# Second MoE layer as Strassen half products in four sum banks, with attention regrouped to 256 queries

## Chip, cores, metric

One Trainium2 chip, one core. The metric is the device time of one execution in microseconds (us); the span in a profile is a little shorter (413.1 against 414.8 here).

## What is computed

Attention over 4 batches of 8 heads of 768 queries (head size 64), then a mixture of 4 experts on the 3072 rows that come out. Three heads are "retrieval" heads (plain causal mask); five are "streaming" heads (4 sink keys and a window of 64).

```python
mask = where(retrieval[h], causal, causal & (is_sink | in_window))
a = softmax(where(mask, q @ k.T / 8, -1e9))          # (4, 8, 768, 768)
x = (a @ v).transpose(0, 2, 1, 3).reshape(3072, 512)
p = probs / (probs.sum(-1, keepdims=True) + 1e-9)    # (3072, 4)
for e in range(4):
    out += p[:, e:e+1] * (relu(x @ w1[e]) @ w2[e])   # 512 -> 1024 -> 512
```

## The kernel before

It works in 8 groups of 384 queries. While TensorE runs the experts of one group, the attention of the next group is threaded through it in small steps. The program fixes the order of instructions on every engine by the order in which it issues them. The kernel divides PSUM, where TensorE's results arrive, into eight banks of 512 fp32 columns: four for scores and first layer, two for attention values, two for the second layer's outputs.

```python
def bank():
    return pA.tile([P, 512], FP32, name="pA", bufs=4)

def scores(h):
    for cols, parts, masks in score_tiles(h):
        # ... matmuls keys x queries into a bank, exp on ScalarE, mask on VectorE
        es_of[h].append((es, parts))
        run_late()                      # products of earlier values, if any wait
        yield ns

def values(h):
    hp, u = divmod(h, 2)
    # ... (first group: other banks, warm-up matmuls)
    ps = pV.tile([P, 512], FP32, name="pV", bufs=2)
    # ... matmuls: values and a column block of ones, so sums stand beside them
    nc.scalar.activation(out=rc[r, :], in_=ps[o, 0:CH], func=AF.Ln, bias=eps[o, :])

    def scale(r=r, ps=ps):
        nc.vector.tensor_tensor(
            out=xT[g][r, hp, :], in0=ps[r, 0:CH], in1=rc[r, :], op=ALU.mult)

    # ... (pairs of the first group cut)
    nc.scalar.activation(out=rc[r, :], in_=rc[r, :], func=AF.Exp, scale=-1.0)
    late.append(scale)                  # issued at the next score step

def moe_group(g):
    for e in range(E):
        # ... layer 1: for each of 8 blocks 4 matmuls of 384 columns, ReLU on ScalarE
        for j in range(3):
            ps_o = pO.tile([P, DM], FP32, name="pO", bufs=2)
            for ft in range(FTP):
                nc.tensor.matmul(out=ps_o, lhsT=hs[:, ft, j * P : (j + 1) * P],
                                 rhs=w2sb[:, e * FTP + ft, :],
                                 start=(ft == 0), stop=(ft == FTP - 1))
            # ... acc = p * ps_o (+ acc) on VectorE, store after the last expert
```

The softmax here doesn't subtract the row's maximum and nothing guards it: scores larger than these inputs give would overflow.

Of the kernel before, what the change touches and what calls it, by code (L numbers as in the profile page):

```python
# [17 lines left out]
def kernel(  # L18
# [28 lines left out]

    nc = tc.nc
# [3 lines left out]
    CH = 3 * P  # L52
# [7 lines left out]
    G = B * NCH  # L60

    RETR = (1, 0, 1, 0, 0, 0, 1, 0)
    RH = [h for h in range(H) if RETR[h]]
    SH = [h for h in range(H) if not RETR[h]]
    NS = int(n_sink)
    NW = int(window)
    TK = 96
    R0 = P - TK
    TQ = TK + NW
    NT = S // TK  # L70
    TC = CH // TK
    assert NS <= R0 and NW == 64 and NS + NW <= TK
    WQ = 55
    WK = WQ + NW - 1
    WT = 7
    WO = P - WK + NW
    assert WT * WQ - 1 == CH and NS + WK <= P

# [3 lines left out]
    pA = ctx.enter_context(tc.tile_pool(name="pA", bufs=1, space=bass.MemoryType.PSUM))  # L82
    pV = ctx.enter_context(tc.tile_pool(name="pV", bufs=1, space=bass.MemoryType.PSUM))
    pO = ctx.enter_context(tc.tile_pool(name="pO", bufs=1, space=bass.MemoryType.PSUM))
# [7 lines left out]
    def bank():  # L92
        return pA.tile([P, 512], FP32, name="pA", bufs=4)


    w1sb = pers.tile([P, E * DMP, F], FP16, name="w1sb")
    w2sb = pers.tile([P, E * FTP, DM], FP16, name="w2sb")
    NR, NSH = len(RH), len(SH)
    kR = []
    kSf = []  # L100
    vR = []
    vSf = []
    for i in range(2):
        kR.append(pers.tile([P, NCH, NR, 3, P], FP16, name=f"kR{i}"))
        kSf.append(pers.tile([P, NCH * TC * NSH * P], FP16, name=f"kS{i}"))
        vR.append(pers.tile([P, S // P, len(RH), P], FP16, name=f"vR{i}"))
        vSf.append(pers.tile([P, NT * NSH * P], FP16, name=f"vS{i}"))
    kS = kSf[0].rearrange("p (c t s x) -> p c t s x", c=NCH, t=TC, s=NSH)
    vS = vSf[0].rearrange("p (t s x) -> p t s x", t=NT, s=NSH)

    def windows(x, c):

        return x[1 - c][:, 0 : WT * NSH * P].rearrange(
            "p (t s x) -> p t s x", t=WT, s=NSH
        )
# [5 lines left out]
    bS = pers.tile([P, 3, TQ], FP16, name="bS")  # L121
    eps = pers.tile([P, 1], FP32, name="eps")
    mC = pers.tile([P, 2 * P], FP16, name="mC")
    mS = pers.tile([P, 4, TQ], FP16, name="mS")
    mW = pers.tile([P, WT + 2, WQ], FP16, name="mW")
# [4 lines left out]


    kRr = pers.tile([P, NR, 3, P], FP16, name="kRr")
    kSr = pers.tile([P, WT, NSH, P], FP16, name="kSr")
    k_sinks = pers.tile([NS, 1, NSH * P], FP16, name="k_sinks")
    v_sinks = pers.tile([NS, 1, NSH * P], FP16, name="v_sinks")

# [5 lines left out]
    def key_tile(b, c, h, t):  # L142

        i = b % 2
        if RETR[h]:
            return kR[i][:, t // 3, RH.index(h), t % 3, :]
        if b:
            return windows(kSf, c)[:, t, SH.index(h), :]
        return kS[:, t // TC, t % TC, SH.index(h), :]

    def v_tile(b, c, h):

        i = b % 2
        if RETR[h]:
            return vR[i][:, :, RH.index(h), :]
        if b:
            return windows(vSf, c)[:, :, SH.index(h), :]
        return vS[:, :, SH.index(h), :]


    q16 = {}

    def rows_of(x, b, h, c):
        return x[b, h, c * CH : (c + 1) * CH, :].rearrange("(j p) d -> p j d", p=P)

    def tiles_of(x, b, h, c):
        return x[b, h, c * CH : (c + 1) * CH, :].rearrange("(t r) d -> r t d", r=TK)

    def windows_of(x, b, h, c):

        assert b > 0
        first = ((b * H + h) * S + c * CH - WO) * D
        return bass.AP(x.tensor, x.offset + first, [[D, P], [WQ * D, WT], [1, D]])

    def load_by_rows(x, x16, b, c):
        for j in range(3):
            s0 = c * CH + j * P
            gp.dma_start(
                out=x16[:, j, :, :],
                in_=x[b, :, s0 : s0 + P, :].rearrange("h p d -> p h d"),  # L180
            )

    def load_q(b, c):
        q16[b, c] = att.tile([P, 3, H, D], FP16, name="q16", bufs=2)
        load_by_rows(q, q16[b, c], b, c)

    def load_triples(x, dst, b, c):

        gp.dma_start(
            out=dst.rearrange("p h j d -> p h (j d)"),  # L190
            in_=x[b, :, c * CH : (c + 1) * CH, :].rearrange(
                "h (p j) d -> p h (j d)", j=3
            ),
        )

    def load_k(b, c):

        for h in range(H):
            if RETR[h]:
                gp.dma_start(  # L200
                    out=kRr[:, RH.index(h), :, own(h)], in_=rows_of(k, b, h, c)
                )
            else:
                gp.dma_start(  # L204
                    out=kSr[:, :, SH.index(h), own(h)],
                    in_=windows_of(k, b, h, c),
                )
# [3 lines left out]
    def alloc_qT(b, c):  # L211
        qTs[b, c] = att.tile([P, HP, CH], FP16, name="qT", bufs=2)

    def put_sinks(x, sinks, c):

        x = x.rearrange("p t s x -> p t (s x)")
        src = sinks
# [211 lines left out]
    for e in range(2, E):  # L429
        load_w1(e, 0, F)  # L430
        load_w2(e)
# [421 lines left out]
```

## Time and profile before

| | before |
|---|---|
| time, median of 3 runs | 414.85 us |
| span of the profiled run | 413.1 us |
| TensorE busy | 395.8 us (96%) |
| VectorE, ScalarE, GpSimd busy | 38%, 58%, 34% |
| mean granted TensorE clock | 0.998 |

The prediction below reads the groups, the chain and the windows. In the profile lines PE is TensorE, PEld its weight loads, DVE VectorE, ACT ScalarE, POOL GpSimd; L728 is line 728 of that run's kernel, so the numbers shift where a run adds lines. Of the tiles, pA is a bank of scores or layer 1, pV a value bank, es the exponentials, rc the reciprocals of their sums, xT the normalised values, hs the hidden activations, sums their sums. Two more views matter for comparing later. First the row of the page that gives the granted TensorE clock in tenths (9 is 90% or more), one digit for each fortieth of the span:

```profile
PEclk9999999999999999999999999999999999999999
```

Second, of the table of waits (engine, line, what it waited for: us in total, times, longest), TensorE's largest and the largest that concerns values:

```profile
PE pA L728 <- ACT hs L741: 2.5, 4, 0.7
PE pV L609 <- DVE es L583: 0.9, 1, 0.9
```

TensorE never waits for a value bank: with two banks, one head's values are written while the other's are read.

### The profile page before, as it was taken

Reading aid. Unit: us, or ns where it says so; the run is one execution under the profiler, and the core shown is the slowest. Engines: PE = TensorE matmul, PEld = TensorE weight load, DVE = VectorE, ACT = ScalarE, POOL = GpSimd, SP = SyncE. Lnnn points to the kernel's source line nnn. Section 1 sums busy time; section 2 is a strip of 40 time slices with the busy share of each in tenths; the row PEclk is TensorE's granted clock in tenths of the full one; section 3 lists DMA queues with packets and bytes.
Section 4 is the critical chain, followed back from the end, with each engine's and each line's share of the span. In section 5 each row is a group of like instructions: output and inputs, shape, how many; then the busy total and the mean of one; then the engine's idle time right before and its main releaser. Section 6 shows DMA issues by size and latency. Waiting matters only on the chain.

```text
span 413.1 us, 6801 instructions
## 1 busy us (share of the span) xinstructions
PE 395.8 (96%) x2670; PEld 222.4 (54%) x2670; DVE 155.8 (38%) x302; ACT 240.9 (58%) x509; POOL 141.7 (34%) x176
## 2 busy tenths in 40 slices
PE   6799999999999999999999999999999999999996
PEld 3565555555555555555555555555555555555552
DVE  7975553223433325233333333233343222432222
ACT  2676874336876547656665448566565477653331
POOL 8938618359359177002930085000000000000000
PEclk9999999999999999999999999999999999999999
DMA  9999999999989999058984999259002000020002
GB/s 173 142 195 204 209 208 133 136 210 124 174 64 181 217 75 101 27 107 147 111 53 96 182 72 77 17 108 166 2 2 76 5 2 0 2 76 2 1 2 76
DMA packets 159988, 40.83 MB, mean 99 GB/s; under 512 B 150364, under 2 KB 154836, under 8 KB 159956
## 3 DMA queue, kind: packets, MB, share of 16 engines
q0 software_dynamic: 102592, 20.98, 59.5%
q1 hardware_dynamic: 54164, 18.62, 21.7%
q10 hardware_dynamic: 3200, 0.79, 0.9%
q8 instruction: 21, 0.34, 0.3%
q14 instruction: 11, 0.09, 0.1%
HBM read 43.57 MB, written 6.29 MB: 121 GB/s over the span
## 4 chain that ended last, share of the span: by engine, by line
PE 86%; ACT 6%; DVE 4%; DMA 2%; issue 1%; ACTq 0%; DVEq 0%
PE pO L749 40%; PE pA L728 36%; PE pV L609 5%; PE pA L561 4%; ACT hs L741 2%; DMA q<-in_q_dram 2%; ACT rc L628 2%; DVE kS L490 1%; ACT rc L638 1%; DVE vS L261 1%; ACT es L579 1%; DVE kR L474 1%; DVE qT L465 0%; PE pO L355 0%; PE pV L355 0%
## 5 line engine op out<-in xcount | busy, mean ns | idle before, releaser
L728 PE MATMUL pA<-xT,w1sb 128*128 128x384 f16 x1024 | 187.4, 326 | 3.9 <-ACT hs L741 2.5
L749 PE MATMUL pO<-w2sb,hs 128*128 128x512 f16 x768 | 180.8, 379 | 0.0
L741 ACT ACTIVATE hs<-pA 128x384 f16<-128x384 f32 x256 | 122.1, 494 | 95.9 <-PE pA L728 89.1
L728 PEld LDWEIGHTS <-w1sb 128*128 128x128 f16 x1024 | 96.8, 98 | 65.5 <-issue 5.5
L749 PEld LDWEIGHTS <-hs 128*128 128x128 f16 x768 | 72.7, 98 | 74.3 <-ACT hs L741 0.6
L765 DVE SCALAR_TENSOR_TENSOR acc<-pO,p_sb,acc 128x512 f32<-128x512 f32 x72 | 53.9, 749 | 99.5 <-PE pO L749 98.9
L579 ACT ACTIVATE es<-pA 128x512 f16<-128x512 f32 (+3 forms) x122 | 61.0, 511 | 22.7 <-PE pA L561 20.9
L628 ACT ACTIVATE rc<-pV,eps 64x384 f32<-64x384 f32 x60 | 34.5, 575 | 33.0 <-PE pV L609 32.0
L204 POOL DMA_DIRECT2D kSr<-in_k_dram x30 | 30.1, 1006 | 36.5 <-issue 14.7
L250 POOL DMA_DIRECT2D vS<-in_v_dram x30 | 30.4, 1024 | 34.8 <-PE pV L609 34.0
L633 DVE TENSOR_TENSOR xT<-pV,rc 64x384 f16<-64x384 f32 x60 | 33.1, 552 | 4.2 <-PE pA L728 1.7
L583 DVE TENSOR_TENSOR es<-es,mW 128x384 f16<-128x384 f16 x30 | 10.8, 360 | 57.2 <-ACT es L579 57.2
L638 ACT ACTIVATE rc<-rc 64x384 f32<-64x384 f32 x58 | 30.2, 521 | 1.8
L761 DVE TENSOR_SCALAR acc<-pO,p_sb 128x512 f32<-128x512 f32 x24 | 18.0, 749 | 34.3 <-PE pO L749 33.0
L200 POOL DMA_DIRECT2D kRr<-in_k_dram x18 | 14.1, 783 | 47.2 <-DMA kR<-kRr 43.2
L583 DVE TENSOR_TENSOR es<-es,mC 128x256 f16<-128x256 f16 (+1 forms) x42 | 10.8, 257 | 45.4 <-ACT es L579 45.0
L561 PE MATMUL pA<-qT,kR 128*128 128x384 f16 (+2 forms) x120 | 25.0, 278 | 0.4
L609 PE MATMUL pV<-es,vR 128*128 128x384 f16 (+2 forms) x120 | 21.6, 278 | 0.0
L246 POOL DMA_DIRECT2D vR<-in_v_dram x24 | 19.2, 800 | 4.3 <-DMA w2sb<-in_moe_w_dram 4.2
L561 PEld LDWEIGHTS <-kS 128*128 128x128 f16 x255 | 13.9, 98 | 9.5 <-issue 2.9
L561 PE MATMUL pA<-qT,kS 128*128 128x55 f16 (+4 forms) x255 | 16.6, 195 | 2.2 <-ACT es L579 1.6
L609 PEld LDWEIGHTS <-vS 128*128 128x128 f16 x255 | 13.2, 98 | 9.1 <-DVE vS L261 3.0
(77 smaller groups left out, 161.3 us busy)
## 6 DMA issues: line engine op xcount, KB each, us to landing
out_dram<-acc SPq DMA_DIRECT2D x24, 256.0 KB
w1sb<-in_moe_w_dram POOLq DMA_DIRECT2D x4, 1024.0 KB, 14.5
w2sb<-in_moe_w_dram POOLq DMA_DIRECT2D x4, 1024.0 KB, 17.5
kSr<-in_k_dram POOLq DMA_DIRECT2D x30, 112.0 KB, 3.8
vS<-in_v_dram POOLq DMA_DIRECT2D x30, 112.0 KB, 3.8
q<-in_q_dram POOLq DMA_DIRECT2D x18, 128.0 KB, 4.4
vR<-in_v_dram POOLq DMA_DIRECT2D x24, 48.0 KB, 4.1
kRr<-in_k_dram POOLq DMA_DIRECT2D x18, 48.0 KB, 4.1
```

Source lines behind the costliest of these rows:

```text
L204: gp.dma_start(out=kSr[:, :, SH.index(h), own(h)], in_=windows_of(k, b, h, c),)
L250: gp.dma_start(out=t[:, :, own(h)], in_=windows_of(v, b, h, c))
L561: nc.tensor.matmul(out=ps[:, o : o + nq], lhsT=key_tile(b, c, h, t), rhs=qTs[b, c][:, hp, q0 : q0 + nq], start=(n == 0 or not first), stop ...
L579: nc.scalar.activation(out=es[:, 0:cols], in_=ps[:, 0:cols], func=AF.Exp, scale=SC)
L609: nc.tensor.matmul(out=ps[:, q0 : q0 + nq], lhsT=v_tile(b, c, h)[:, t, :], rhs=es[:, o : o + nq], start=(n == 0), stop=(n == len(work) - 1 ...
L628: nc.scalar.activation(out=rc[r, :], in_=ps[o, 0:CH], func=AF.Ln, bias=eps[o, :])
L633: nc.vector.tensor_tensor(out=xT[g][r, hp, :], in0=ps[r, 0:CH], in1=rc[r, :], op=ALU.mult)
L638: nc.scalar.activation(out=rc[r, :], in_=rc[r, :], func=AF.Exp, scale=-1.0)
L728: nc.tensor.matmul(out=pss[ft][:, 0:CH], lhsT=w1sb[:, e * DMP + ct, ft * P : (ft + 1) * P], rhs=xT[g][:, ct, :], start=(ct == 0), stop=(ct ...
L741: nc.scalar.activation(out=hs[:, ft, :], in_=ps[:, 0:CH], func=AF.Relu)
L749: nc.tensor.matmul(out=ps_o, lhsT=hs[:, ft, j * P : (j + 1) * P], rhs=w2sb[:, e * FTP + ft, :], start=(ft == 0), stop=(ft == FTP - 1),)
L765: nc.vector.scalar_tensor_tensor(out=acc[nt], in0=ps_o, scalar=p_ap, in1=acc[nt], op0=ALU.mult, op1=ALU.add,)
```

## The change

**Intent.** Strassen's scheme multiplies 2x2 blocks with seven half products in place of eight. The products are summed over the four experts in PSUM, so the additions that combine them are done once per group, not once per expert. For that the probability has to be in the hidden activations (scaled at the eviction of layer 1, on VectorE, one bank in four on ScalarE and GpSimd). Four banks hold the running sums through a whole group. Groups become 256 queries (2 x 128 rows), streaming heads use 52-query tiles, and all attention after the second group stays at fp16 loads and DMA transposes. The first two of twelve groups use a plain second layer while the weights' sums are made.

The eight banks are now three for scores and first layer, one for values, four for sums. Two heads share the value bank, 256 columns each. The core of the diff (cuts marked):

```diff
-    CH = 3 * P
+    NJ = 2
+    CH = NJ * P
...
-        return pA.tile([P, 512], FP32, name="pA", bufs=4)
+        return psum.tile([P, 512], FP32, name="pA", bufs=3)
+    def bank_v():
+        return psum.tile([P, 512], FP32, name="pV", bufs=1)
+    def bank_m(i):
+        return psum.tile([P, 512], FP32, name=f"pM{i}", bufs=1)
... attention, values of a head
+            if u == 0:
+                run_late()
+                ps_of[hp] = bank_m(hp - 1) if first and hp else bank_v()
+            ps = ps_of[hp][:, u * CH : (u + 1) * CH]
...
+            if u == 1:
+                # ... two logarithms, one exponential on ScalarE
+                def normalise(x=ps_of[hp], rc=rc):
+                    for w in (1, 0):
+                        r = rows[w]
+                        nc.vector.tensor_tensor(
+                            out=xT[g][r, hp, :], in0=x[r, w * CH : (w + 1) * CH],
+                            in1=rc[r, :], op=ALU.mult)
+                late.append(normalise)
... layer 1, eviction
+                    if i == 0:
+                        nc.scalar.activation(out=tmp, in_=ps, func=AF.Relu)
+                        gp.tensor_tensor(out=h4, in0=tmp4, in1=p4, op=ALU.mult)
+                    else:
+                        nc.vector.scalar_tensor_tensor(
+                            out=h4, in0=ps4, scalar=0.0, in1=p4,
+                            op0=ALU.max, op1=ALU.mult)
... sums of the hidden activations, per expert
+        add(hs[:, :, P:CH], hs[:, :, 0:P], s[:, 0:2], ALU.subtract)   # 1024 columns
+        add(hs[:, 0:FH, :], hs[:, FH:FTP, :], s[:, 2:4])              # 1024 columns
+        add(hs[:, 0:FH, 0:P], hs[:, FH:FTP, P:CH], s[:, 4])           # 512 columns
... second layer: 7 x 4 matmuls of 256 columns
+        m52, m34, m76, m1 = sum_banks[g]
+        for n, step in enumerate(steps):
+            for ps, half, a, b in step:
+                for f in range(FH):
+                    nc.tensor.matmul(out=ps[:, half * HD : (half + 1) * HD],
+                        lhsT=a(f), rhs=b(f),
+                        start=(e == 0 and f == 0 and half == 0),
+                        stop=(e == E - 1 and f == FH - 1))
+            if e == E - 1:
+                way_out(g, n)          # copies and five additions, one store
... order of a cycle
+    merge(plain(0, 0, 3), PLAIN_NS, 1, 0.0, 0.9)   # attention of group 1 beside one expert
+    # then seven plain experts with the attention of group 2, then per group:
+            yield from in_turns(layer1_scaled(g, 0), layer2(last, 2))
+            ...
```

## The prediction

> **What bounds the kernel now.** I read the page first (busy shares, groups), then the chain of work that ended last in order of time, then TensorE's timeline for the pitch of single matmuls, then ten-microsecond windows, then the timelines of the first 26 us and of the end.
>
> From the page, the busy shares and the two largest groups (columns: engine, busy us, share, instructions; line, operation, operands, count, busy us and mean ns, idle before):
>
> ```profile
> PE 395.8 (96%) x2670; PEld 222.4 (54%) x2670; DVE 155.8 (38%) x302; ACT 240.9 (58%) x509; POOL 141.7 (34%) x176
> ...
> L728 PE MATMUL pA<-xT,w1sb 128*128 128x384 f16 x1024 | 187.4, 326 | 3.9 <-ACT hs L741 2.5
> L749 PE MATMUL pO<-w2sb,hs 128*128 128x512 f16 x768 | 180.8, 379 | 0.0
> ...
> L765 DVE SCALAR_TENSOR_TENSOR acc<-pO,p_sb,acc 128x512 f32<-128x512 f32 x72 | 53.9, 749 | 99.5 <-PE pO L749 98.9
> ...
> L633 DVE TENSOR_TENSOR xT<-pV,rc 64x384 f16<-64x384 f32 x60 | 33.1, 552 | 4.2 <-PE pA L728 1.7
> ```
>
> TensorE is busy for 96% and its two MoE lines have next to no idle before them; VectorE is at 38%. The mean of a matmul includes its pipeline, so the cost has to come from pitches. The chain in order of time (start, length, what) gives them over unbroken runs, and the timeline gives the short ones:
>
> ```profile
> 70.54 5.20 PE pA L728 x32
> ...
> 121.31 1.73 PE pO L749 x8
> ```
> ```profile
> 122.88 0.36 PE L609 MATMUL pV<-es,vS 128*128 128x54 f16 x7
> 123.08 1.24 PE L749 MATMUL pO<-w2sb,hs 128*128 128x512 f16 x5
> ...
> 162.43 0.38 PE L561 MATMUL pA<-qT,kR 128*128 128x256 f16 x2
> 162.65 0.59 PE L749 MATMUL pO<-w2sb,hs 128*128 128x512 f16 x2
> ```
>
> So 384 columns cost 5.20/32 = 162.5 ns, 512 columns 216 ns, 256 columns 0.22/2 = 110 ns, and seven 54/55-column matmuls start within 0.20 us, 28.6 ns each. That is columns/2.4 + 2.6 ns, with a floor near 28.6 ns. The windows (span; busy us and count of PE, PEld, DVE, ACT, POOL; clock; DMA) show where TensorE is not full:
>
> ```profile
> 50.00:60.00 10.00, 9.13 (x70) 5.41 (x69) 6.33 (x14) 7.84 (x17) 1.74 (x2) 1.00 1.18 210
> ...
> 170.00:180.00 10.00, 10.00 (x64) 5.51 (x63) 3.56 (x6) 5.66 (x12) 1.02 (x1) 1.00 0.39 91
> ...
> 400.00:410.00 10.00, 8.96 (x48) 4.41 (x45) 2.25 (x3) 3.35 (x7) 0.00 (x0) 1.00 0.15 54
> ```
>
> From 70 us to 400 us it is full but for about 3 us in all. Pricing every matmul of the instruction order with the pitches gives 389.4 us (166.5 first layer, 165.8 second, 50.6 attention, 5.2 warm-up, 1.3 for the second half of fp32 transposes, three of which take 0.33 us in the timeline). So of the 413.1 us span 23.7 is TensorE without work: 10.3 before the first MoE matmul at 24.3 us, 9.2 between there and 408.9, and 4.2 after the last matmul. The time reported is 1.75 above the span.
>
> **What the skill says.** "TensorE: Matmul & The Clock Gate", section "Wait — 56ns, not 53.3ns?": start to start N/2.4 plus about 2.5 ns warm, and a floor near 25 ns for small N. The trace agrees on the first (162.5, 216) and shows 28.6 on the second. "VectorE: DVE Perf Modes", section "The perf-mode tier table": a 16-bit tensor_tensor in SBUF runs two elements a cycle, any with a PSUM operand one. The trace agrees: the fp16 mask products take 291 ns at 256 columns and 360 at 384 (0.54 ns a column), the 512-column fp32 operation on PSUM 749. "GPSIMD Engine Reference", section 3.1: a GpSimd tensor_tensor of 2048 fp32 took 4497 ns; no such operation is in this trace. "SBUF — State Buffer", section "SBUF: two separate sides": a VectorE operation with two SBUF inputs and a GpSimd operation reading SBUF exclude each other; not shown by this trace either, and it bears on the new sums against the new GpSimd multiply.
>
> **The change, part by part.**
>
> *Second layer.* Ten of twelve groups (the first two stay plain) take 7 x 4 half products of 256 columns per expert in place of 16 x 512: 10 x 4 x 28 x 109.2 ns = 122.3 us, against 640 x 216 = 138.2. That is -15.9. The seven-eighths rule would give -17.3; the 2.6 ns on twice as many matmuls takes the rest.
>
> *First layer.* The same columns in 1536 matmuls of 256 instead of 1024 of 384: 167.8 against 166.5, +1.3.
>
> *Attention.* Retrieval has the same columns in more matmuls. The streaming heads of the first batch go from 160-column tiles to five 48/52-column ones, at the floor of 28.6. Priced like before: 47.7 against 50.6, less 2.9; fp32 transposes +0.6. Warm-up 1.5 against 5.2, less 3.7.
>
> TensorE's work is then 369.0, against 389.4: -20.4. All of this is on the path, since TensorE sets the end. The rest of the question is how much idle comes with it.
>
> *Prologue.* Its 256 queries need less VectorE work, and VectorE set its length: busy with few gaps from 5.6 us on. After: kR 3 x 0.42, kS 5 x 1.0 (three pieces each), sinks 1.6, qT 1.25, value sinks 2.0, xT 8 x 0.42, together 14.5 us, by 0.15 us plus 1.04 ns a column from the 384-column rows. I take the first MoE matmul at 19.5 instead of 24.3. TensorE's work before it is 6.6, so 12.9 idle (+2.6).
>
> *First stage.* All of group 1's attention goes beside one expert of group 0, 12.9 us of TensorE. VectorE has there: kR 1.3, kS 5 x 0.8, qT 1.7, masks 2.3, sinks 1.5, xT 3.4, hs and output 4 x 0.75, small things 2.3 = 19.5 us. Group 1's first layer waits for the last xT: 6.5 idle.
>
> *Weight sums.* Four times five fp16 operations of 1024 columns. Four of them 0.69 us and one perhaps at one element a cycle, 1.2: 4.0 us each time. The first layer's second bank queues behind them; TensorE gets about 3.9 us ahead before it needs that bank, and it comes at 4.8. About 1.0 each, 4.0 idle.
>
> *Steady groups.* TensorE per group: 4 x 3.50 + 4 x 3.06 + 3.7 attention = 29.9 us. VectorE: twelve scaled evictions of 0.75 = 9.0, four sets of sums of 1.8 (0.69 + 0.69 + 0.42) = 7.2, masks 2.3, xT 3.4, way out 3.2 = 25.1, so 84%. ScalarE about 14. GpSimd about 18 us of DMA issue plus four multiplies of (an estimate from the GPSIMD page) 1.2. VectorE is under TensorE but in bursts: around the way out it owes some 7 us in 7.5, with three banks for layer one and scores. I allow 0.5 per group, 5.0 in all, against about 3 before.
>
> *Tail.* After the last matmul come two 256-column adds, one 512-column add and one 512 KB store, where before there was one 0.75 us operation and 256 KB. 4.2 + 1.0 + 0.8 = 6.0.
>
> Sum: 369.0 + 12.9 + 6.5 + 4.0 + 5.0 + 6.0 = 403.4 of span, and 405.1 with the 1.75 of before. Prediction 405.0, 2.4% less.
>
> **Rivals.** (1) *VectorE becomes the bound.* The sums' inputs are strided in 128-column runs, where the mask products were whole rows. If that drops them to one element a cycle a set takes 1.22 + 1.22 + 0.69 = 3.1 us, VectorE gets 30.3 us a group against 29.9, and every burst shows: +5 to +12, 410 to 417. For it: 84% leaves little. Against: the mode asks for unit step, which these runs have. (2) *The single value bank makes attention wait.* Before, two banks alternated; now two heads share one, and the next pair waits for two Ln (0.47 each), Exp (0.4), two xT products (0.84) and their place in VectorE's queue: 2.2 to 4 us. Where both scores between are streaming heads there is about 1.7 to 3 us of other work. 0.5 to 1 us per group more: 410 to 413. (3) *GpSimd is late with its multiply,* stuck behind a load that waits for the transposes. The waits of before have kRr loads waiting 43.2 us in five places. The sums then wait and hold the evictions behind them. The transposes now start at 72% of a cycle, 8.4 us ahead, for about 7.5 us of transposes scaled from before (4.0 + 1.3 + 5.2 by tile counts); +3 to +10 if it fails. (4) *The idle I added is smaller,* because the order of work in the first stage overlaps better than a plain sum of VectorE: 5 to 7 less, 398.
>
> **Range and chances.** The -20.4 of TensorE work is near certain, to 1 us. The idle, +10.7 in my sum, may be +4 (398.5) or, with one of rivals 1 to 3 in full, +19 (413). The range is 398.5 to 413. The 2% line is 406.55, so 405.0 lies just inside faster. That the bank count and steady load look deliberately fitted moves me a little that way: faster 0.60, same 0.34, slower 0.06.
>
> **What would show it.** Right: the chain is TensorE at L667 and L824 with x8 runs of 0.87 us; first MoE matmul near 19.5; a gap of some 6 us in TensorE's work before 42 us; VectorE near 80% in windows after 110 us with TensorE at 9.5 or more of 10; the 128x1024 sums near 0.69 us. Wrong: sums of 1.2 us or more; TensorE waiting in L667 for VectorE's eviction (L704) or in L569 for L596 by more than 10 us in total; GpSimd's multiply taking over 2 us or idling behind DMA. If TensorE's busy time falls by 20 but the span by less than 5, a rival is the cause and the waits will name it.

## The result

The changed kernel is correct and takes **477.33 us** (median of 4 runs, 476.42 to 478.86) against 414.82 us for the kernel before. The ratio is 1.152 (95% interval 1.148 to 1.157). Ratios here are the mean time of one kernel's fast runs over that of the other's of the same rounds, so not quite the ratio of the medians quoted. The prediction said 405.0, so the direction is wrong too.

From the page of the changed kernel: busy time, the clock row, and groups that answer to those shown of before (L667 is layer 1, L704 the scaled eviction, L569 the values, L596 the product that normalises values and so frees their bank):

```profile
PE 400.5 (84%) x3724; PEld 328.0 (69%) x3724; DVE 317.1 (67%) x596; ACT 168.7 (35%) x359; POOL 237.4 (50%) x280
...
PEclk9565799999999989999999999989999999989999
...
L667 PE MATMUL pA<-xT,w1sb 128*128 128x256 f16 x1536 | 204.4, 281 | 10.0 <-DMA w1sb<-in_moe_w_dram 3.5
L704 DVE SCALAR_TENSOR_TENSOR hs<-pA,pb 128x512 f16<-128x512 f32 x120 | 81.7, 685 | 61.6 <-PE pA L667 61.4
...
L569 PE MATMUL pV<-es,vR 128*128 128x256 f16 (+1 forms) x140 | 23.9, 273 | 35.1 <-DVE xT L596 33.5
...
L596 DVE TENSOR_TENSOR xT<-pV,rc 64x256 f16<-64x256 f32 x90 | 38.0, 422 | 13.5 <-ACT rc L591 12.3
```

TensorE fell from 96% to 84% busy. Layer 1 hardly waits (10.0 us in 1536 matmuls), but the values wait 35.1 us, of which 33.5 for the normalising product. VectorE is at 67%; in the ten steady groups it is busy for 244.2 of 346.3 us, so 24.4 a group where 25.1 were predicted: it has no more work than expected, only more time. The table of waits says the same, over all shapes:

```profile
POOL hs L698 <- ACT tmp L697: 169.8, 37, 26.1
...
PE pV L569 <- DVE xT L596: 38.8, 23, 2.7
PEld L569 <- issue: 38.5, 24, 2.2
...
DVE kR L444 <- POOL kR L276: 6.9, 1, 6.9
```

The first of these lines is idle time of an engine that has nothing to do and costs nothing. The second is the new wait: 23 times, up to 2.7 us. The weight loads of the same line stand still with it. The last belongs to the first 60 us.

**One such wait, on three engines.** TensorE's timeline (start, length, line, operation; in brackets the idle time before it and what ended it):

```profile
247.52 0.29 PE L569 MATMUL pV<-es,vS 128*128 128x48 f16 x5
...
251.58 1.04 PE L667 MATMUL pA<-xT,w1sb 128*128 128x256 f16 x8
254.37 0.33 PE L569 MATMUL pV<-es,vR 128*128 128x256 f16 x2 [1.75 <-DVE xT L596]
```

ScalarE's timeline of the same stretch:

```profile
247.85 0.95 ACT L586 ACTIVATE rc<-pV,eps 64x256 f32<-64x256 f32 x2 [3.10 <-PE pV L569]
248.83 0.42 ACT L591 ACTIVATE rc<-rc 128x256 f32<-128x256 f32 x1
```

And VectorE's:

```profile
249.60 0.69 DVE L704 SCALAR_TENSOR_TENSOR hs<-pA,pb 128x512 f16<-128x512 f32 x1 [1.18 <-PE pA L667]
250.39 1.63 DVE L713 TENSOR_TENSOR sums<-hs 128x1024 f16<-128x1024 f16 x3
252.66 0.69 DVE L704 SCALAR_TENSOR_TENSOR hs<-pA,pb 128x512 f16<-128x512 f32 x1 [0.63 <-PE pA L667]
253.36 0.86 DVE L596 TENSOR_TENSOR xT<-pV,rc 64x256 f16<-64x256 f32 x2
```

The values of a pair end at 247.8. Logarithms and exponential are done at 249.25, so both products could start. VectorE takes an eviction, the sums, and then stands idle for 0.63 us, waiting for the bank that TensorE is just filling (251.58 to 252.62). It evicts that bank and only then runs the products, which give the value bank back at 254.22. TensorE has reached the next pair's values at 252.62 and waits 1.75 us. The bank was held for 6.4 us, of which 2.3 were needed (0.95 + 0.42 + 0.86, with little between).

This pair is the worst one. Over the 36 pairs of the steady groups the trace gives 2.3 to 6.4 us from the end of the values to the end of the second product, 4.4 in the median. In 9 pairs the products stood behind an eviction, as here (15.8 us of TensorE's idle time just before the next values), in 18 behind the mask product of the next score tile (16.9 us), and in 9 they ran as soon as the exponential was done (none).

**Where the time stands.** Counting layer-1 matmuls along TensorE's timeline marks the stages: no. 0 is the first MoE matmul, no. 32 group 1's first, no. 256 the first of the ten steady groups. The end of the steady groups is taken at the start of the last matmul; by its modelled end the tail is 6.2 us.

| | predicted | measured | more |
|---|---|---|---|
| first MoE matmul at | 19.5 | 22.6 | +3.1 |
| group 1's layer 1 at | 38.9 | 60.3 | +21.4, the 3.1 included |
| from there to the steady groups | 58.7 | 62.6 | +3.9 |
| ten steady groups | 299.8 | 346.3 | +46.5 |
| after the last matmul | 6.0 | 6.5 | +0.5 |
| span | 403.4 | 475.7 | +72.3 |

Of the steady excess, little is the clock: it averaged 0.98 over the ten groups, and 2% of 346.3 us is at most 7 us.

**The first 60 us.** Windows of ten microseconds (span; busy us and count of PE, PEld, DVE, ACT, POOL; clock; DMA share; GB/s), one early, one steady:

```profile
30.00:40.00 10.00, 4.84 (x23) 3.08 (x24) 4.63 (x10) 2.29 (x7) 10.00 (x23) 0.51 0.94 131
...
250.00:260.00 10.00, 8.25 (x81) 7.21 (x80) 6.00 (x12) 1.95 (x4) 2.88 (x3) 1.00 1.15 168
```

The steady one has TensorE at 8.25 of 10 at full clock, and no other engine above 7.21 (weight loads, its own). Between 30 and 40 us TensorE has 4.84 at half the clock, and only GpSimd is full. TensorE's timeline there shows links of half a microsecond to several, most of them ended by another engine:

```profile
22.64 4.40 PE L667 MATMUL pA<-xT,w1sb 128*128 128x256 f16 x20 [3.46 <-DMA w1sb<-in_moe_w_dram]
27.73 0.55 PE L437 MATMUL pA<-ident,x32k 128*128 128x128 f32 x3 [0.69 <-ACT hs L686]
32.81 0.66 PE L478 MATMUL pA<-ident,x32q 128*128 128x128 f32 x2 [4.54 <-issue]
...
35.04 0.59 PE L520 MATMUL pA<-qT,kR 128*128 128x256 f16 x2 [0.58 <-ACT es L538]
...
54.59 0.61 PE L569 MATMUL pV<-es,vS 128*128 128x48 f16 x10 [2.69 <-DVE xT L596]
```

The gap of 4.54 us marked "issue" has its cause in GpSimd's timeline: the zero fills of key tiles stand behind loads of values, and one of those waited for a weight load:

```profile
29.19 0.88 POOL L199 DMA_DIRECT2D vS<-in_v_dram  x1 [5.57 <-DMA w2sb<-in_moe_w_dram]
30.07 0.44 POOL L276 MEMSET kR<- 128x384 f32 x1
```

VectorE's copy into those tiles, which empties the bank of the transposes, waited 6.9 us for the fill (the last line of the waits above). What that was worth is tested below.

### The profile page after: what moved, and what is told of

It is laid out like the page before. It is cut to its first block, busy times and chain, and to the rows that moved or that the text cites. A ratio compares the mean times of both kernels' runs of the same rounds, so it can differ in the third digit from the quotient of the medians.

```text
span 475.7 us, 9400 instructions
## 1 busy us (share of the span) xinstructions
PE 400.5 (84%) x3724; PEld 328.0 (69%) x3724; DVE 317.1 (67%) x596; ACT 168.7 (35%) x359; POOL 237.4 (50%) x280
## 3 DMA queue, kind: packets, MB, share of 16 engines
q1 hardware_dynamic: 75480, 26.55, 28.6%
## 4 chain that ended last, share of the span: by engine, by line
PE 66%; DVE 16%; ACT 7%; issue 6%; DMA 2%; POOL 2%; DVEq 0%; POOLq 0%; ACTq 0%
PE pA L667 30%; PE pM L824 21%; PE pM L728 6%; DVE xT L596 5%; PE pV L569 5%; PE pA L520 3%; DVE hs L704 3%; ACT rc L586 3%; DVE sums L713 2%; DMA w1sb<-in_moe_w_dram 2%; DVE o L713 2%; ACT es L538 1%; ACT tmp L697 1%; ACT rc L591 1%; POOL vS L199 1%
## 5 line engine op out<-in xcount | busy, mean ns | idle before, releaser
L667 PE MATMUL pA<-xT,w1sb 128*128 128x256 f16 x1536 | 204.4, 281 | 10.0 <-DMA w1sb<-in_moe_w_dram 3.5
L667 PEld LDWEIGHTS <-w1sb 128*128 128x128 f16 x1536 | 150.8, 101 | 35.1 <-issue 9.6
L698 POOL TENSOR_TENSOR hs<-tmp,pb 128x512 f16<-128x512 f32 x40 | 55.8, 1394 | 181.9 <-ACT tmp L697 169.8
L704 DVE SCALAR_TENSOR_TENSOR hs<-pA,pb 128x512 f16<-128x512 f32 x120 | 81.7, 685 | 61.6 <-PE pA L667 61.4
L824 PEld LDWEIGHTS <-sums 128*128 128x128 f16 x800 | 76.3, 98 | 8.4
L538 ACT ACTIVATE es<-pA 128x512 f16<-128x512 f32 (+2 forms) x132 | 60.3, 470 | 56.9 <-PE pA L520 51.0
L713 DVE TENSOR_TENSOR sums<-hs 128x1024 f16<-128x1024 f16 (+1 forms) x120 | 77.0, 696 | 3.2
L586 ACT ACTIVATE rc<-pV,eps 64x256 f32<-64x256 f32 x90 | 42.2, 469 | 87.5 <-PE pV L569 86.7
L824 PE MATMUL pM<-w2x,sums 128*128 128x256 f16 x480 | 65.4, 272 | 0.0
L569 PE MATMUL pV<-es,vR 128*128 128x256 f16 (+1 forms) x140 | 23.9, 273 | 35.1 <-DVE xT L596 33.5
L191 POOL DMA_DIRECT2D kSr<-in_k_dram x50 | 44.6, 904 | 15.9 <-DMA kS<-kSr 8.1
L596 DVE TENSOR_TENSOR xT<-pV,rc 64x256 f16<-64x256 f32 x90 | 38.0, 422 | 13.5 <-ACT rc L591 12.3
L569 PEld LDWEIGHTS <-vR 128*128 128x128 f16 x144 | 13.6, 102 | 42.5 <-issue 34.9
L824 PEld LDWEIGHTS <-hs 128*128 128x128 f16 x320 | 29.9, 97 | 3.3
```

Of the source, the lines that this page charges most:

```text
L191: gp.dma_start(out=kSr[:, :, SH.index(h), own(h)], in_=tiles_of(k, g, h))
L538: nc.scalar.activation(out=es[:, 0:cols], in_=ps[:, 0:cols], func=AF.Exp, scale=SC)
L569: nc.tensor.matmul(out=ps[:, q0 : q0 + nq], lhsT=value_tile(g, h, t), rhs=es[:, o : o + nq], start=(n == 0), stop=(n == len(work) - 1), sk ...
L586: nc.scalar.activation(out=rc[rows[w], :], in_=ps_of[hp][x, w * CH : (w + 1) * CH], func=AF.Ln, bias=eps[x, :],)
L596: nc.vector.tensor_tensor(out=xT[g][r, hp, :], in0=x[r, w * CH : (w + 1) * CH], in1=rc[r, :], op=ALU.mult,)
L667: nc.tensor.matmul(out=pss[i][:, n * CH : (n + 1) * CH], lhsT=w1sb[:, e * DMP + ct, ft * P : (ft + 1) * P], rhs=xT[g][:, ct, :], start=(n ...
```

## The experiments

Eighteen kernels ran, beside runs of the kernel before on the same chip. The stage marks of each come from counting as above; where an expectation says 62.9 for group 1's first layer, it means the point from which that layer runs on (its first three matmuls start at 60.3, then it waits 1.7 us). My theories in order: (A) the single value bank delays attention in the steady groups; (B) VectorE's load from the new sums is the cause; (C) the first stage is too crowded, by fills, banks or links; later, for A, whether the bank's own chain or the place of its last two instructions holds it.

### Is it the value bank, or VectorE's load?

**Two value banks** (wrong: the first product is summed into another's bank, relative error 1.06).

```diff
-        return psum.tile([P, 512], FP32, name="pV", bufs=1)
+        return psum.tile([P, 512], FP32, name="pV", bufs=2)
-            sum_banks[g] = [bank_m(i) for i in range(4)]
+            sum_banks[g] = [bank_m(i) for i in range(3)]     # m1 = m52
```

> Wrong on purpose: M1 is summed into the bank of M5 and M2, and the PSUM bank so freed becomes a second bank for attention's values. Matmuls, evictions and sums stay in number and size. Theory (in the steady groups TensorE waits for the one value bank, because the products that free it stand in VectorE's queue behind sums and evictions): the waits of L569 for L596 (38.8 us) nearly vanish and a steady group takes 31 to 33 us in place of 34 to 36; total 440 to 455 us. Rival (VectorE's load as such holds TensorE): the waits move to the first layer's banks (L667 for L704), and the total stays over 468.

Measured: 447.76 us, ratio 1.082 (1.074 to 1.091). The wait of L569 for L596 is down to 0.5 us (once); the steady stretch fell from 346.3 to 316.2. So 30 of the 46.5 us hang on the bank.

**Without the hidden sums** (wrong, relative error 1.41: the products read the plain activations).

```diff
     def hidden_sums(g, e):
+        return
-        by_rows = s[:, 2:4, :] ...
+        by_rows = hs[:, 0:FH, :]                              # diff, both_ alike
```

> Wrong on purpose: the sums of hidden rows are left out and the second layer reads the hidden rows themselves. This takes some 77 us of VectorE's 317 away and GpSimd's contention with them; the single value bank stays. If the queue in front of the products is the cause: most of the waits of L569 for L596 go as well, since what stands in front of them is sums, total 445 to 458. If the wait is the bank's own chain (Ln, Ln, Exp, two products) with or without a queue: little falls, 468 to 476.

Measured: 476.53 us, 1.152. VectorE's busy time fell from 317.1 to 244.9 us and nothing else moved. Its table of waits:

```profile
PE pV L569 <- DVE xT L596: 37.0, 22, 2.7
```

Theory B is refuted: 72 us less work on VectorE, of 244 in the steady groups, change nothing, and the wait for the bank does not depend on the sums: the bank is held for 4.4 us in the median as before. By what I had set down, this spoke for the chain's own length. The products at once, below, show that it was not that either.

**Groups and banks of the change, but a plain second layer.**

```diff
     for g in range(2, G):
-            cycle(g), total, g + 1, 0.0, 0.93,
+            plains(g), total, g + 1, 0.0, 0.93,     # plain(g, e) for four experts
```

> Half of the change undone: groups of 256, 52-query tiles and the single value bank stay, the second layer is plain everywhere, its output scaled as before, no sums, no scaled evictions. TensorE work is about 385 us, 16 above the changed kernel. If Strassen's extra work for VectorE is what lost the gain: 430 to 445 (early loss stays, steady groups near full). If the regrouped attention is: 470 to 490, with the waits of L569 for L596 as before.

Measured: 468.9 us, 1.133 (1.126 to 1.141), with 26.9 us (20 times) of the same wait. Most of the loss is there without any Strassen: the regrouped attention with its one value bank costs it. Strassen itself adds 8 us to that, where the prediction had its second layer save 15.9: what comes with it costs some 24 us in this setting. A plain second layer with the products at once was not run, so whether Strassen pays at all once the bank is out of the way stays open.

**The freed bank given to scores and layer 1 instead** (wrong, as with two value banks): four of those, one for values.

```diff
-        return psum.tile([P, 512], FP32, name="pA", bufs=3)
+        return psum.tile([P, 512], FP32, name="pA", bufs=4)
```

> Wrong on purpose, as the run with two value banks: M1 is summed into the bank of M5 and M2. The freed bank goes to scores and first layer (four instead of three), and attention keeps one value bank. If the value bank is the cause and not banks as such: little, 468 to 476, with the waits of L569 for L596 still over 30 us. If any bank would do: 445 to 455.

Measured: 473.4 us, 1.144 (1.138 to 1.151):

```profile
PE pV L569 <- DVE xT L596: 40.6, 22, 2.7
```

So it is not banks as such: the same bank is worth 30 us as a value bank and 4 here.

**The kernel before with one value bank** from its second group on.

```diff
-                ps = pV.tile([P, 512], FP32, name="pV", bufs=2)
+                if not first:
+                    run_late()
+                ps = pV.tile([P, 512], FP32, bufs=1,
+                    name="pVf" if first and (h // 2) % 2 else "pV")
```

> The kernel before, with one value bank instead of two from its second group on, everything else as it was (correct result). If a lone value bank costs by its own chain of Ln, Exp and product, here about 0.58 + 0.52 + 0.55 = 1.65 us a head against what TensorE has to do before the next head's values: up to 1 us for many of 56 heads, total 425 to 450. If the cost in the changed kernel came from its fuller VectorE: within 5 us of 414.

Measured: 441.17 us against 414.8, 1.065 (1.059 to 1.070). The wait appears in the old kernel too:

```profile
PE pV L614 <- DVE xT L638: 27.4, 22, 2.6
```

### What holds the bank: its chain, or its place in the order?

**ScalarE copies the values out** as fp16, and VectorE multiplies from the copy.

```diff
+                if not first:
+                    val = att.tile([P, CH], FP16, name="val", bufs=1)
+                    for w in (0, 1):
+                        nc.scalar.copy(out=val[rows[w], :],
+                            in_=ps_of[hp][rows[w], w * CH : (w + 1) * CH])
```

> Correct result. From group 1 on ScalarE copies the two halves of the value bank to fp16 in SBUF, and one VectorE product of 128x256 from SBUF takes the place of two of 64x256 from PSUM. The bank is then free after four ScalarE operations (two Ln of 0.47, two copies of 0.37, about 1.7 us) and waits for no place in VectorE's queue. If the bank's release is what costs the steady groups: most of the 29 us that two banks gave, total 446 to 458. If it is VectorE's load (denied by the run without sums): about 470 or more.

Measured: 453.45 us, 1.097 (1.092 to 1.102), correct. Steady stretch 322.2. Only three waits of values for the bank are left, now on ScalarE's copy:

```profile
PE pV L569 <- ACT val L595: 3.8, 3, 2.2
```

This frees the bank without VectorE, but does not tell which part of VectorE's share mattered.

**That copy, and a fourth bank for scores and layer 1** (wrong, as before).

> Wrong on purpose in the same way. A fourth bank for scores and first layer, and ScalarE frees the value bank (453.5 us by itself). If the rest of the steady excess is three banks shared by scores and first layer: the steady groups, 322 us from their start to the last matmul in that run, come to 304 to 310, total 435 to 442. If the rest is something else: 448 to 455.

Measured: 445.54 us, 1.077 (1.068 to 1.086). Steady 314.6 against 322.2 with the copy alone: three banks in place of four cost another 7.6 us once the value bank is out of the way. Both the steady stretch and the total missed what was expected (304 to 310, 435 to 442), so three banks are only a part of what is left.

**The products at once.** One line: they are issued right after the exponential, not put off.

```diff
-                late.append(normalise)
+                normalise()
```

> The two products that give the value bank back are put into VectorE's order right after the values of a pair, not just before the next pair's values. If the place in VectorE's order is what holds the bank, the wait of the values matmul for the products (38.8 us in 23 places) falls to under 10 and the steady stretch from 346 to 318-328; VectorE then stands in line for the exponential, so waits of the first layer for the scaled eviction should appear, 2 to 10 us in all. Time 450 to 465. If the length of the chain itself (two logarithms, exponential, two products) holds it, the wait stays above 25 us and the time within 1% of 477.

Measured: **443.53 us**, 1.074 (1.071 to 1.077), correct. The steady stretch fell from 346.3 to 314.0, with one value bank as in the change. The waits of TensorE for the bank:

```profile
PE pV L569 <- DVE xT L596: 3.2, 5, 1.3
```

ScalarE's and VectorE's timelines at one pair of values, which ended at 217.5:

```profile
217.56 0.95 ACT L586 ACTIVATE rc<-pV,eps 64x256 f32<-64x256 f32 x2 [4.00 <-PE pV L569]
218.55 0.42 ACT L591 ACTIVATE rc<-rc 128x256 f32<-128x256 f32 x1
```
```profile
219.00 0.86 DVE L596 TENSOR_TENSOR xT<-pV,rc 64x256 f16<-64x256 f32 x2 [1.74 <-ACT rc L591]
```

The bank is back at 219.86, 2.3 us after the values, and TensorE's next values start at 225.84 without a wait. Over the 36 pairs the bank is held for 2.3 us in the median, at most 3.7. VectorE now stands still for the exponential (37.5 us in 32 places in the whole run), and that costs next to nothing: the waits of layer 1 for scaled evictions that I expected (2 to 10 us) did not come, and time and steady stretch are better than expected. So the **place in the order** was the cause, not the chain's length. In the first group the same edit hurts: the first MoE matmul starts at 26.8 instead of 22.6.

**The products 1.6 us of issued work later.**

```diff
                 late.append(normalise)
+                pend.append((now[0], late, normalise))   # issued by tick() in merge
```

> The same products are put into VectorE's order once 1.6 us of TensorE's work have been issued after the values, about when the exponential is ready (0.95 us of logarithms and 0.42 us of exponential). If the place in the order is the cause, the wait for the products falls under 10 us without VectorE standing in line, steady stretch 312 to 322, time 445 to 456, so as good as the copy by ScalarE (453.5) or better. If the chain's length is the cause, no change: 470 to 480.

Measured: 461.64 us, 1.116 (1.113 to 1.119), correct: half of the gain.

```profile
PE pV L580 <- DVE xT L607: 24.0, 19, 2.7
```

I missed: putting the products where the exponential should be ready leaves them behind mask products, evictions and sums that were issued in between (in the trace, 26 of 36 pairs start more than 0.3 us after their exponential). Standing in line early is the better choice here.

**The input scaled instead of the output** (with ScalarE's copy): x times p once per expert, a plain ReLU after (and the first two of a cycle's turns swapped).

```diff
+        nc.vector.tensor_tensor(out=xs_of[g, e], in0=xT[g], in1=p4, op=ALU.mult)
-                            rhs=xT[g][:, ct, :],
+                            rhs=x1[:, ct, :],
```

> Correct result. On top of the run before: the probabilities scale the first layer's input (one fp16 product of 128x1024 on VectorE per expert, about 0.7 us) in place of scaling its output, so evictions become plain Relu, two on ScalarE and two on VectorE per expert; three evictions of 0.69 and a GpSimd multiply less per expert, one product and one more eviction on ScalarE. VectorE some 2 to 3 us less per group. If what is left in the steady groups after the bank is VectorE's bursts: 6 to 12 us faster than the run before. If not: within 3 us of it.

Measured: 481.37 us, 1.164 (1.159 to 1.168), a miss. VectorE has less to do, but a cycle's first layer now needs the whole attention output and its product with p before it starts (the long waits stand at the first layer-1 matmul of a cycle):

```profile
PE pA L693 <- DVE xs L675: 32.7, 13, 5.0
```

It gave one useful figure by the way. With no GpSimd multiply beside them, the third hidden sum takes 419 ns (first block, this experiment), against 714 in the change (second block), by the groups with shapes kept apart:

```profile
L723 DVE TENSOR_TENSOR sums<-hs 128x512 f16<-128x512 f16 x40 | 16.7, 419 | 0.0
```
```profile
L713 DVE TENSOR_TENSOR sums<-hs 128x512 f16<-128x512 f16 x40 | 28.6, 714 | 0.0
```

And in the run without the sums GpSimd's multiply took 1260 ns in place of 1394. They lengthen each other, off the path: within the trace of the change, the 22 such sums with no multiply beside them took 418 ns on average, the 18 with one 1076.

### The first 120 microseconds

**Fills first:** the two zero fills ahead of the loads.

```diff
+    fill(gp, kR[1], 0.0)
+    fill(gp, kS[1], 0.0)
     load_w2(0)
     for h in range(H):
         load_v(1, h)
-    fill(gp, kR[1], 0.0)
-    fill(gp, kS[1], 0.0)
```

> The two zero fills of group 1's key tiles are moved on GpSimd ahead of the second weight load and group 1's value loads, behind which they ended at 31.9 us. Theory (early loss is a chain: GpSimd blocked at a load, so late fills, so late keys of group 1, so TensorE idle and its clock down): VectorE's 6.9 us wait for the fill goes, group 1's first layer starts at some 50 to 55 us in place of 62.9, total 465 to 471 us. Rival (group 1's attention, packed beside one expert, is bound by its own VectorE and ScalarE steps or by the weight loads): the start moves by less than 3 us, total 474 to 478.

Measured: 474.77 us, 1.148 (1.139 to 1.157). Group 1's first layer starts 4.3 us earlier, the steady groups 2.9, the end 1.6: most is given back. TensorE's gap of 4.54 us marked "issue" is down to 1.46.

**Fill-in matmuls,** to keep the clock up: `warm_up(ps_warm, 4, 512)` before values and transposes of group 1.

> Correct result. Matmuls on zeros go into TensorE's gaps: four of 256 columns ahead of each pair of values in the prologue, four of 512 at each step of group 1's attention, as the kernel before had in its prologue. The clock from 10 to 60 us should rise from 0.5 to 0.7 to about 0.9. Theory (the early stage is a chain of VectorE, ScalarE and single transposes and short matmuls, in which TensorE's slow clock doubles its links): group 1's first layer starts 3 to 6 us earlier than at 62.9. Rival (the clock is a consequence and the chain is elsewhere): less than 2 us, or later.

Measured: 479.68 us, 1.160. The clock rose:

```profile
PEclk9867989999999999989999999989999999999999
```

Group 1's first layer starts at 58.7 against 60.3 and the steady groups at 122.9 as before. Between the first two marks the clock rose from 0.64 to 0.81, and that bought 1.6 us: the low clock is more a consequence of the waits than their cause. What the fill-in matmuls themselves cost there was not separated.

**Group 2's attention begun later** (at 0.6 of its stretch in place of 0.4, with fills first).

> Correct result. The early fills of the first run, and group 2's attention begins at 60% instead of 40% of the seven plain experts. In the first run group 1's first layer came 4.3 us earlier and the total only 2.6: if the rest was given back because group 2's attention then met keys whose transposes had not landed (5.1 us of weight loads waiting for kS), the total is now 468 to 473; if not, 473 to 478.

Measured: 475.27 us, 1.150 (1.143 to 1.157): no gain, so a later start alone does not keep what the fills gave.

**Alternate value banks in group 1's attention,** with one of the sum banks that is idle then.

```diff
+                elif g == 1 and hp % 2:
+                    ps_of[hp] = bank_m(3)
```

> Correct result. In the early stage alone, group 1's attention takes its values in turn in the value bank and in one of the four sum banks, which is idle then; steady groups keep their single bank. In the changed kernel group 1's first layer starts at 60.3 us. If the single value bank lengthens that stage as well (two banks everywhere gave 54.4): 54 to 56 us, and a total of 471 to 475, as part of what comes earlier is given back. If not: 59 to 61.

Measured: 479.76 us, 1.157. Group 1's first layer starts at 53.0, 7.3 earlier, but the steady groups at 124.7. The bank holds that stage too, but the next stage then waits for other things; what exactly I did not isolate.

**Group 1's attention beside two experts** in place of one, with fills first and the second expert's weights loaded earlier.

```diff
-    merge(plain(0, 0, 3), PLAIN_NS, 1, 0.0, 0.9)
+    merge(two(), 2 * PLAIN_NS, 1, 0.0, 0.9)      # plain(0, 0, 3), then plain(0, 1)
```

> Correct result. Group 1's attention lies beside two experts of group 0 instead of one; the fills come first and the second expert's first-layer weights ahead of group 1's values. Theory: that stage is a chain of TensorE, VectorE and ScalarE links of about a microsecond in which TensorE has nothing else; a second expert (7 us) then fits into its gaps nearly free. The steady groups' start (122.9 us in the changed kernel, 120.0 with the fills alone) comes to 112 to 116, total 466 to 471. Rival: the early stage is bound by the weight and key transfers (transfers fill the first 118 us): the start stays at 118 to 122.

Measured: 471.38 us, 1.137 (1.133 to 1.142). The steady groups start at 113.3, 9.6 earlier, but the steady stretch took 348.9 (462.2 less 113.3) and so a part was lost again. As the fills alone gave 2.9, the spread gave some 6.6. The crowding of that one expert is the larger part of the early loss that I could undo.

### Together

**ScalarE's copy, alternate banks and the spread stage.**

> Correct result. Three changes together: ScalarE frees the value bank, two value banks in group 1's attention, and the spread of that attention. If the gains are separate: 453.5 of the first alone less 6 to 9 for the start, 443 to 448. It does not reach the 414 of the kernel before.

Measured: 444.97 us, 1.073 (1.069 to 1.076), as expected.

**The same, with keys and queries of group 2 loaded ahead of the third expert's weights,** because scores waited 5.3 us for its transposed keys.

```diff
     def later_loads():
-        load_w1(2)
-        load_w2(2)
         ...
+        load_w1(2)
+        load_w2(2)
```

> Correct result. On the run with three changes together (445.0): group 2's keys and queries are loaded ahead of the third expert's weights, and their transposes are asked for at once. If the early gain is given back to keys that land late: the 5.3 us wait for kS at 87 us goes, the steady groups start at 106 to 110 instead of 114.2, total 437 to 442. If the transfers as a whole are the limit, the third expert's weights are late in turn: 443 to 448.

Measured: 442.07 us, 1.069 (1.057 to 1.081). That wait is down to 2.6 us, the steady groups start at 112.3 against 114.2, later than expected, and the gain in time is not clear of the noise.

**The same without ScalarE's copy, the products at once** from the second group on.

> The products at once from the second group on (in the first group as in the change, where at-once made the first MoE matmul start at 26.8 instead of 22.6), with the earlier repairs of the first 120 us: attention of the second group beside two experts, alternate value banks there, fills and keys early; no copy by ScalarE. If the early and the steady parts add, the steady stretch starts near 112 us, lasts 312 to 316 and the time is 432 to 438. If the early repairs are given back once the steady part is faster (its loads and transposes come due earlier), waits of the scores for the transposed keys grow past 10 us and the time stays at 440 to 445.

Measured: **434.05 us**, 1.049 (1.044 to 1.054), correct, the best version of the changed kernel. The steady groups start at 114.2 (8.7 earlier than in the change) and take 311.7 (34.6 less), so the two repairs add. Its page and its waits:

```profile
PE 392.6 (91%) x3724; PEld 326.0 (75%) x3724; DVE 318.8 (74%) x596; ACT 168.6 (39%) x359; POOL 242.9 (56%) x280
```
```profile
PE pV L574 <- DVE xT L601: 2.1, 4, 1.2
```

No version beat the kernel before.

| kernel | us | ratio to before |
|---|---|---|
| the change | 477.33 | 1.152 |
| products at once | 443.53 | 1.074 |
| products by time | 461.64 | 1.116 |
| ScalarE's copy | 453.45 | 1.097 |
| two value banks (wrong result) | 447.76 | 1.082 |
| spread first stage | 471.38 | 1.137 |
| spread, alternate banks, keys early, ScalarE's copy | 442.07 | 1.069 |
| spread, alternate banks, keys early, products at once | 434.05 | 1.049 |

## Why the prediction was wrong, step by step

**TensorE's work, -20.4: right as far as the runs can tell.** Runs of eight 256-column matmuls lie 0.87 us apart (246.65 to 247.52 in the timeline), as priced, and 28 matmuls of 256 columns take the place of 16 of 512. (The prediction's parts add to -20.6, by rounding; and 52-column matmuls start 25.9 ns apart in the changed kernel, not 28.6.) With these pitches a steady cycle of the change holds 29.9 us of work on average, the number that was predicted. It did not fail; it was outweighed.

**Steady groups, 0.5 us of idle each: the step that failed most.** The stretch took 4.6 us a group more than with these 0.5 (46.5 in ten). It is the sign of being wrong that the prediction itself set down, L569 waiting for L596 by more than 10 us: it was 38.8. The prediction named the mechanism as its second rival, "the single value bank makes attention wait", and listed the parts of the chain and "their place in VectorE's queue". It sized it at 0.5 to 1 us per group. The wait is about 3 us per group: 30 of the 46.5 are gone with a second bank (316.2) and 32 with the products at once (314.0), with no bank added. What the estimate lacked: "2.2 to 4 us" was the time to release the bank. The chain by itself needs 2.3, but the trace shows 4.4 in the median and up to 6.4, because the program puts the products off to the next step of scores or to just before the next pair's values. There they come behind a mask product that waits for the next scores (18 of 36 pairs) or behind the eviction of the bank that TensorE filled last (9), so TensorE often arrives first. The prediction does not mention this deferral. The kernel before defers too; there a second bank hides it, and with one bank it shows at once (27.4 us of waits, +26 us). VectorE follows its order strictly: the Trainium skill says so ("PSUM — Partial Sum Buffer", section "Engine vs sequencer instructions": ScalarE, VectorE and GpSimd queues are strict first in, first out), and the trace agrees: at 252.0 VectorE stood idle for 0.63 us, with both products ready behind the eviction that it waited for.

What is left of the steady excess is 314.0 against 299.8. A fourth bank for scores and first layer was worth 7.6 us beside ScalarE's copy; whether it is worth the same beside the products at once was not run. The other half is open; small waits for transposed keys, for evictions and for exponentials are in the tables, none of those above 5.0 us in all in that run.

**First stage, 6.5 us of idle: mis-sized.** The prediction summed VectorE's work there (19.5 us) beside TensorE's 12.9, as if each engine's work could run without gaps. It took 37.7 us from the first MoE matmul to group 1's. The attention of a whole group beside one 7-us expert is a chain of short links across four engines, with few banks and one value bank. The experiments give parts: the fills behind loads 4.3 us, alternate value banks 7.3, but both mostly given back later. Spreading it over two experts, with the fills first, brought the steady groups 9.6 us nearer, and all repairs together 8.7 (114.2 against 122.9) with the products at once, 10.6 with ScalarE's copy, so the early repairs do not add to each other. The other 15 to 17 us to the predicted 97.6 stay open; transfers are busy at nearly their full share in most of the first 120 us, and I did not separate that from the links. The first MoE matmul came 3.1 us late, for a wait of 3.5 us for its weights that I had not counted.

**Weight sums, 4.0 idle:** the stage was 3.9 us longer than predicted; not separated further. The one operation of unsure speed took 1219 ns, as estimated (1.2).

**VectorE's durations: right in sum, in part by luck.** The 24.4 us a group against 25.1 hide errors that offset each other. Scaled eviction 685 ns (predicted 750), sums of 1024 columns 687 (690). The sum of 512 columns took 714, not 420, because GpSimd's multiply lay beside 18 of the 40; mask products of 256 columns took 390 and 492 ns, not 291; GpSimd's multiply took 1394, not 1200. All of that is off the path. (The prediction's 749 ns for VectorE on PSUM is of a scalar_tensor_tensor; for tensor_tensor, its 552 ns at 384 columns is the evidence.)

**Tail, 6.0:** 6.5 from the start of the last matmul, 6.2 from its end. Right.

**The rivals.** VectorE as the bound: refuted (244.9 us busy in place of 317.1, same time). The single bank: right mechanism, mis-sized by a factor of three to six. GpSimd late: its multiply waits for ScalarE, and only two waits on the sums (12.1 us) show at all; a run without the multiply was slower, though it changed more than that. Less idle than summed: the opposite came.

**The chances.** The range went up to 413 with "one of rivals 1 to 3 in full", so the mis-sized rival bounded it. Slower by over 2% had 0.06.

## What to carry to other kernels

When a change takes away a spare buffer, ask not only how long the release chain is but where the program issues its last instruction: put off behind work that waits for the same engine that will need the buffer, it comes late (here in 27 of 36 pairs). Moving that instruction costs one line (here 7% of the time), so try it before buying a bank or moving work to another engine. And a sum of work per engine is only the least that a stage can take in which short steps on four engines wait for each other (here 19.4 us predicted, 37.7 measured): spread such a stage over more of the independent work.

## What the Trainium skill lacked or had wrong

- "Perfetto Trace Analysis", section "Optimization Strategy", says that consistent bubbles can mean too little SBUF or PSUM for the next tile. The bubbles were here (23 waits, 38.8 us) and a second bank did remove them, but so did a change of order with the same bank (3.2 us left). The page does not name the place of the releasing instruction in an engine's order as a cause.
- "PSUM — Partial Sum Buffer", section "Summary: rules for kernel authors", says to evacuate promptly, without a size. In these runs one value bank in place of two cost 30 us in the changed kernel and 26 in the kernel before, and in the changed kernel 2.3 against 4.4 us of holding the bank (medians) decided it.
- "VectorE: DVE Perf Modes", section "The perf-mode tier table", has no row for scalar_tensor_tensor. With fp16 SBUF operands it took 1219 ns for 1024 columns, against 687 for tensor_tensor of the same size.
- "SBUF — State Buffer", section "SBUF: two separate sides", was said in the prediction to be unseen. The runs agree with it: the 512-column sum takes 418 ns with no multiply of GpSimd beside it and 1076 with one; the multiply 1260 ns without the sums and 1394 in the kernel that has them.
- "TensorE: Matmul & The Clock Gate", section "Wait — 56ns, not 53.3ns?", gives a floor near 25 ns between small matmuls. In the changed kernel 52-column ones start 25.9 ns apart on average, so the floor holds as the least; 54- and 55-column ones start some 28 ns apart in the kernel before, more than the floor.
